# Expert 0's first tile built from one-hot products and an early gather, and routing groups of 4 and 2 tiles, in an attention, mixture-of-experts and feed-forward chain

## The chip, the cores and the metric

The kernel runs on one core of one Trainium2 chip. The metric is the device time of one execution in microseconds (us), the median of several runs; less is better. Times inside the kernel come from one profiled execution and count from its first instruction.

## The reference

```python
attn = softmax(q @ k.T / 8 where 0 <= i - j < 64) @ v      # 4 x 8 x 576 x 64
x = attn as rows                                             # 2304 x 512
compute = x @ w_skip > 0                                     # the other rows stay as they are
e = argmax(x @ w_gate); gate = softmax(x @ w_gate)[e]        # 8 experts
x = x + gate * (relu(x @ w1[e]) @ w2[e])                     # 512 -> 1024 -> 512
h = x @ w_in                                                 # 512 -> 2048
g = h if h >= 1, 0 if h <= -1, else (h + 1) ** 2 / 4
out = g @ w_out                                              # 2048 -> 512
```

All arrays are fp32. With the inputs of the test the experts get 63, 85, 141, 113, 265, 116, 58 and 62 rows.

## The kernel before

The work has three stages, one behind the other, and the program text is the order on every engine.

**Attention and routing (0 to about 110 us).** The 2304 rows are 18 tiles of 128 tokens. Each tile t goes through the score products (`stage_s`, L338, softmax on VectorE and ScalarE), the transposes of the weights (`stage_t`, L363, copied to pts by ScalarE and VectorE, L367 and L369), the value products (`stage_v`, L388, which read v from the four buffers vt and end in x, scaled by VectorE at L394 to L396), a store of x to DRAM (x1), the transposes of x (`stage_x`, L409), and the gate products (`stage_l` L430, `stage_l2` L449). The loop runs them as a pipeline, several tiles at a time; the last tiles are written out by hand behind it (L642 to L696). Tiles are routed in six groups of three (`ROUTES`). `route_a` (L457 to L470, six VectorE operations) chooses each token's expert as a one-hot row oh; `route_b` (L484 to L519) ranks tokens within the expert by products of triangular and ones matrices, on top of the counts so far (run); `route_h` (L547, L549) makes from a rank two one-hot matrices (to, at), `route_c` (L564) multiplies them and adds up (acc, in the end idx at L571), the list of row numbers by expert and slot; `route_g` (L530 to L533) makes the gate and stores it beside x in x1, from ScalarE's queue. 120 spare products of ones (`keep_warm`, L444) stand among the last groups' steps, in batches of 6, 14, 20 and 80; 69 (L586) stand at the start of the program.

**Experts (116.5 to 271 us).** `fetch` gathers 128 rows of x1 with their gates by an indirect DMA of POOL (L715; an expert's tile t with column e·18+t of idx), `prep` transposes them (L733) and splits them into a high and a low half (L131 ScalarE, L132 VectorE), `ffn` does the two products (L759 ha and hb, L798 y) in three passes of high and low halves, `store_x` writes the rows back by an indirect DMA of POOL (L724), with small memsets (tick) that keep scatters and gathers apart. Every expert has a first tile; the second and the third run inside `tc.If` on the counts, which each engine reads into registers (L833, cnt_i). `fetch(e, 2)` stands at the start of the second tile. Expert e's hooks, called within `ffn`, prepare the next expert and split weights.

**Weights.** They come as raw tiles (L115 wu, L118 wd), at most `most` at a time, from SP's or ScalarE's queue, and ScalarE (L136) and POOL or VectorE (L137) split each into a pair in a ring of 14. Before, `most` is 2 in the loop and 6 from t = 14 on, so that raw loads go out while attention still loads vt from SP's queue (L305).

**Dense stage (271 to 701 us).** Six blocks of 384 rows, products L922 and L950 one behind the other.

## Time and profile before

| | |
|---|---|
| runs of the kernel | 708.78, 703.59, 702.24 us; median 703.59 |
| the profiled execution | 703.17 us, of which 701.5 are the span from the first to the last instruction |
| TensorE busy | 674.2 us of the span, 96% |
| VectorE, ScalarE, POOL busy | 425.6, 385.9, 90.7 us |
| mean granted TensorE clock | 0.992 |
| first product of expert 0 (ha) | 116.53 us |
| start of the dense stage | 271.35 us |

In rows of the timeline the first number is the start and the second the length in us; then engine, line, operation, the tiles written and read, the number of instructions, and in brackets the idle time of the engine before it and what ended it. PE is TensorE, PEld its weight loads, DVE VectorE, ACT ScalarE; an engine's name with a q is its sequencer, which issues DMAs. [...]

### The profile page before, as it was taken

The numbers are of one execution on the slowest core, as the hardware profiler recorded it, in microseconds if no ns is written. First come the engines' busy times: TensorE is split into PE (matmuls) and PEld (weight loads), VectorE is DVE, ScalarE is ACT, GpSimd is POOL, SyncE is SP. The second block draws the span as 40 slices with busy tenths as digits, with TensorE's granted clock in tenths as the row PEclk, the third lists the DMA queues.
The fourth block names the chain that finished last, engine by engine and source line by source line (L and its number), as shares of the span: only waits on it lengthen the run. The fifth ranks groups of instructions, "written<-read, shape, count | busy, mean of one in ns | idle before, by whom it ended". The sixth has DMA issues, their size and how long they took to land.

```text
span 701.5 us, 12250 instructions
## 1 busy us (share of the span) xinstructions
PE 674.2 (96%) x4630; PEld 575.6 (82%) x4630; DVE 425.6 (61%) x808; ACT 385.9 (55%) x768; POOL 90.7 (13%) x137
## 2 busy tenths in 40 slices
PE   7999989999998998999999999999999999999997
PEld 6777778776776765987989999999999999999995
DVE  4888864897781799787888854444433433433332
ACT  5887742583751764566766655454444454445443
POOL 3255545222210221000000000000000000000000
PEclk9999998999999999999999999999999999999999
DMA  8999953897891693442333202121300030001001
GB/s 259 288 272 290 307 133 115 289 329 275 267 357 31 205 332 95 172 127 84 121 92 96 69 0 61 31 60 31 91 1 0 1 91 0 1 1 45 1 1 45
DMA packets 34504, 88.83 MB, mean 127 GB/s; under 512 B 6958, under 2 KB 8110, under 8 KB 34420
## 3 DMA queue, kind: packets, MB, share of 16 engines
q1 hardware_dynamic: 26208, 73.82, 34.3%
q10 hardware_dynamic: 5892, 7.35, 3.1%
q0 software_dynamic: 2320, 6.58, 2.8%
q8 instruction: 48, 0.79, 0.5%
q14 instruction: 36, 0.29, 0.1%
HBM read 75.65 MB, written 13.12 MB: 127 GB/s over the span
## 4 chain that ended last, share of the span: by engine, by line
PE 55%; DVE 3%; ACT 1%; issue 1%; ACTq 0%; DVEq 0%
PE h L922 27%; PE po L950 26%; PE spare L1038 1%; PE p2x L912 1%; DVE c L943 1%; DVE c L940 1%; ACT q L933 1%; DVE w L137 1%; DVE gs L941 0%; DVE q L932 0%; DVE x2T L132 0%; ACT q L929 0%; DVE q L936 0%; ACT part L959 0%; ACT w L136 0%
## 5 line engine op out<-in xcount | busy, mean ns | idle before, releaser
L922 PE MATMUL h<-x2T,w 128*128 128x384 f32 x1152 | 218.0, 337 | 1.1 <-DVE x2T L132 0.9
L950 PE MATMUL po<-w,gs 128*128 128x512 f32 x864 | 217.3, 395 | 1.7 <-ACT w L136 0.9
L922 PEld LDWEIGHTS h<-x2T,w 128*128 128x128 f32 x1152 | 204.6, 188 | 10.0 <-DVE x2T L132 1.7
L950 PEld LDWEIGHTS po<-w,gs 128*128 128x128 f32 x864 | 159.5, 188 | 32.3 <-ACT w L136 1.2
L929 ACT ACTIVATE q<-h 128x384 f32<-128x384 f32 x96 | 47.0, 489 | 108.1 <-PE h L922 104.2
L932 DVE TENSOR_SCALAR q<-q 128x384 f32<-128x384 f32 x96 | 34.4, 358 | 98.2 <-ACT q L929 98.0
L936 DVE TENSOR_TENSOR q<-hs,q 128x384 f32<-128x384 f32 x96 | 53.7, 559 | 49.8 <-ACT q L933 49.8
L938 ACT ACTIVATE gs<-q 128x384 fp32r<-128x384 f32 x96 | 50.4, 525 | 60.0 <-DVE q L936 60.0
L941 DVE TENSOR_TENSOR gs<-q,gs 128x384 fp32r<-128x384 f32 x96 | 53.6, 559 | 44.4 <-ACT gs L938 44.4
L136 ACT ACTIVATE w<-raw 128x1024 fp32r<-128x1024 f32 x64 | 65.3, 1056 | 18.7 <-PEq L869 4.7
L798 PE MATMUL y<-w,hT 128*128 128x512 f32 x264 | 70.2, 403 | 4.1 <-DVE hT L132 2.8
L137 DVE TENSOR_TENSOR w<-raw,w 128x1024 fp32r<-128x1024 f32 x55 | 64.8, 1219 | 3.8 <-ACT w L136 1.9
L933 ACT ACTIVATE q<-q 128x384 f32<-128x384 f32 x96 | 50.5, 526 | 22.2 <-DVE q L932 18.6
L798 PEld LDWEIGHTS y<-w,hT 128*128 128x128 f32 x264 | 47.3, 188 | 17.3 <-DVE hT L132 4.5
L349 ACT ACTIVATE pr<-s,nb 128x128 f32<-128x128 f32 x144 | 39.2, 384 | 16.5 <-DVE nb L345 16.5
L931 ACT ACTIVATE hs<-h 128x384 f32<-128x384 f32 x96 | 46.7, 487 | 0.0
L759 PE MATMUL ha<-w,mxT 128*128 128x512 f32 x132 | 35.3, 416 | 3.7 <-ACT mxT L131 1.5
L759 PEld LDWEIGHTS ha<-w,mxT 128*128 128x128 f32 x132 | 25.1, 197 | 13.2 <-issue 4.5
L759 PE MATMUL hb<-w,mxT 128*128 128x512 f32 x132 | 35.2, 402 | 0.0
L345 DVE TENSOR_REDUCE nb<-s 128x4 f32<-128x512 f32 x36 | 23.2, 686 | 16.0 <-PE s L338 14.5
L724 POOL DMA_INDIRECT x<-mx,idx x11 | 16.5, 1501 | 115.6 <-POOLq L865 60.4
L131 ACT ACTIVATE hT<-hTp 128x512 fp32r<-128x512 f32 x22 | 13.2, 599 | 27.1 <-PE hTp L772 13.0
(170 smaller groups left out, 702.1 us busy)
## 6 DMA issues: line engine op xcount, KB each, us to landing
raw<-in_wu SPq DMA_DIRECT2D x61, 512.0 KB, 6.0
raw<-in_wd SPq DMA_DIRECT2D x31, 512.0 KB, 4.0
x<-x SPq DMA_DIRECT2D x22, 256.0 KB, 3.2
vt<-in_vs SPq DMA_DIRECT2D x36, 130.0 KB, 6.2
out<-out SPq DMA_DIRECT2D x36, 128.0 KB, 2.4
x<-x ACTq DMA_DIRECT2D x17, 256.0 KB, 6.6
q<-in_qs SPq DMA_DIRECT2D x8, 512.0 KB, 5.0
kt<-in_ks SPq DMA_DIRECT2D x8, 512.0 KB, 6.2
```

Of the source, the lines that this page charges most:

```text
L136: nc.scalar.activation(t[:, 0], src, AF.Copy)
L137: eng.tensor_tensor(t[:, 1], src, t[:, 0].bitcast(F32), ALU.subtract)
L759: nc.tensor.matmul(ph, lhsT=xT[:, a, c, :], rhs=halves[4 * e + j, c][:, b, :], start=(n == 0), stop=(n == len(seq) - 1),)
L798: nc.tensor.matmul(py, lhsT=hT[j][:, a, c, :], rhs=halves[4 * e + 2 + j, c][:, b, :], start=(j == 0 and n == 0), stop=(j == 1 and n == len ...
L922: nc.tensor.matmul(ph, lhsT=halves[U_IN + m // 4, c][:, b, (m % 4) * P : (m % 4 + 1) * P], rhs=xT[:, a, c, :], start=(n == 0), stop=(n == ...
L929: nc.scalar.activation(q, ph, AF.Relu, bias=0.5, scale=0.5)
L931: nc.scalar.activation(h, ph, AF.Copy)
L933: nc.scalar.activation(q, q, AF.Square)
L936: nc.vector.tensor_tensor(q, h, q, ALU.max)
L938: nc.scalar.activation(gs[:, 0], q, AF.Copy)
L941: dve.tensor_tensor(gs[:, 1], q, gs[:, 0].bitcast(F32), ALU.subtract)
L950: nc.tensor.matmul(po[i], lhsT=gs[:, a, i * P : (i + 1) * P], rhs=w[:, b, :], start=(m == m0 and (a, b) == PASSES[0]), stop=(m == m1 - 1 a ...
```

## The change

Expert 0's first tile no longer waits for idx and a gather. Its transposed rows are summed in one PSUM bank (mpx_0, tag s0) from fp32 products. For tiles 13 to 17 x is still in SBUF (13 and 14 in a part of kt that is free by then): `add_rows` multiplies it with a selector, the one-hot matrix of "this token has rank j in expert 0" (`choose`). For the first 13 tiles the rows come by an indirect gather of POOL that is issued as soon as the first four groups' list stands (`gather_ahead`), into a buffer set to zero before, and are added by a product with the identity.

For this the groups are 3, 3, 3, 4, 2 and 3 tiles (`ROUTES`), and the fourth group, tiles 9 to 12, is routed between the value products of tile 15 and the transposes of tile 16. All spare products of the routing's end go. The 69 warm products of ones, bf16, 108 columns, become 11 of the identity, fp32, 192 columns. `most` is 2 until t = 14, then 3, and 6 only behind the last gates, where the loads go out from ScalarE's queue. The counts are read on each engine ahead of the split of expert 0's tile; expert 1's gather goes out before expert 0's (which still brings its rows for the sum at its end), and VectorE's next weight splits stand behind both. `fetch(e, 2)` moves from the start of the second tile into the first tile's hook, right behind the second tile's transposes.

```diff
-ROUTES = (3, 3, 3, 3, 3, 3)
-WARM = 69
-WARM_COLUMNS = 108
+ROUTES = (3, 3, 3, 4, 2, 3)
+WARM = 11
+WARM_COLUMNS = 96
-KEEP = (14, 20, 80, 6, 36)
+KEEP = 36
+KEPT_AT = {13: (2, 0), 14: (2, 512)}
+ROWS_AT = (0, 0)
+SEL_AT = ((1, 0), (1, 128), (1, 256), (1, 384), (1, 512))
...
+        def choose(t, i):
+
+            sel = kept(*SEL_AT[t + i - t0], P)
+            nc.vector.tensor_scalar(
+                sel, slot_r[:, 0], st["ps", t][:, i : i + 1], 0.0, op0=ALU.add, op1=ALU.is_equal
+            )
+            return sel
+
+        def gather_ahead():
+
+            at = sm.tile([P, 1], I32, tag="ahead", name="ahead", bufs=1)
+            nc.vector.tensor_copy(at, acc[:, 0:1])
+            nc.gpsimd.indirect_dma_start(
+                out=rows, out_offset=None, in_=x1[0 : t0 * P], in_offset=bass.IndirectOffsetOnAxis(ap=at, axis=0),
+                bounds_check=t0 * P - 1, oob_is_err=False,
+            )
+
+        def add_rows(px, x, sel, first=False, last=False):
+            for c in range(KD):
+                nc.tensor.matmul(
+                    px[:, c, :], lhsT=x[:, c * P : (c + 1) * P], rhs=sel,
+                    start=(first and c == 0), stop=(last and c == KD - 1),
+                )
...
-        warm = psp.tile([P, P], F32, tag="o", name="warm")
+        warm = psp.tile([P, H, P], F32, tag="o", name="warm")[:, 0:2, 0:WARM_COLUMNS]
         for _ in range(WARM):
-            nc.tensor.matmul(warm[:, 0:WARM_COLUMNS], lhsT=ones, rhs=ones[:, 0:WARM_COLUMNS], start=True, stop=True)
+            nc.tensor.matmul(
+                warm, lhsT=ident, rhs=ident[:, 0:WARM_COLUMNS].rearrange("p (o k) -> p o k", o=1).to_broadcast([P, 2, WARM_COLUMNS]),
+                start=True, stop=True,
+            )
...
-            most[0] = 1 if t < 3 else 2 if t + 4 < NT else RAWS[0] + RAWS[1]
+            most[0] = 1 if t < 3 else 2 if t + 3 < NT else 3
...
         stage_x(NT - 4)
+        tp, (ip, m, side) = of[NT - 6][0], of[NT - 6][1:]
+        assert ip == m - 1 and not due and not gates
+        route_a(tp, m)
         stage_v(NT - 3)
         store_t(NT - 3, nc.sync)
+        route_b(tp, m, side)
+        route_g(tp, m)
+        route_h(tp, m, range(1, m))
+        route_h(tp, m, [0], dve)
         stage_t(NT - 2)
         stage_t(NT - 1)
-        ranks[0]()
         stage_v(NT - 2)
...
         stage_x(NT - 3)
-        stage_l(NT - 4)
+        stage_l2(NT - 4, *of[NT - 4][1:])
+        n0, n = ROUTES[-2:]
+        route_a(t0, n0)
         stage_x(NT - 2)
+        route_c(tp, m)
+        gather_ahead()
         stage_x(NT - 1)
...
+        route_b(t0, *of[t0][2:])
+        sels = [choose(t0, i) for i in range(n0)]
         stage_l(NT - 3)
...
-        keep_warm(KEEP[3])
         stage_l2(NT - 1, *of[NT - 1][1:])
-        route_g(t0, of[t0][2])
-        for f in later:
-            f()
+        route_p(t0, n0)
+        route_h(t0, n0)
         route_a(t1, n)
-        route_h(t0, of[t0][2], [n - 1])
+        x0 = bank("s0", "mpx0_0")
+        for i in range(n0):
+            add_rows(x0, xs_late[t0 + i], sels[i], first=(i == 0))
+        route_g(t0, n0)
         route_g(t1, n)
-        keep_warm(KEEP[0])
+        most[0] = RAWS[0] + RAWS[1]
+        load_raws(nc.scalar)
         route_b(t1, *of[t1][2:])
-        route_h(t1, n)
-        route_c(t0, of[t0][2])
+        add_rows(x0, rows, ident)
+        sels += [choose(t1, i) for i in range(n)]
+        nc.vector.tensor_tensor(cnt_i, st.pop("cn"), base[:, 0], ALU.subtract)
+        for i in range(n):
+            add_rows(x0, xs_late[t1 + i], sels[n0 + i], last=(i == n - 1))
+        route_p(t1, n)
+        route_h(t1, n, [0])
+        route_h(t1, n, range(1, n), dve)
+        route_c(t0, n0)
         route_c(t1, n)
...
+        _, counts = nc.values_load_multi_w_load_instructions(cnt_i[0:1, 0:NE], min_val=0, max_val=N)
+        xeT[0, 0] = prep(None, "0_0", px=x0)
+        fetch(1, 0)
         fetch(0, 0)
 
         nc.gpsimd.memset(tock, 0.0)
         nc.vector.tensor_copy(tick_seen, tock)
         work(splits, [dve] * 2)
-        pre(0, 0)
...
-        _, counts = nc.values_load_multi_w_load_instructions(cnt_i[0:1, 0:NE], min_val=0, max_val=N)
...
                     prep(xe[e, 1], f"{e}_1", "mxTl", xeT[e, 1])
+                    fetch(e, 2)
...
             with tc.If(counts[e] > P):
-                fetch(e, 2)
                 tile_of(e, 1)
```


Three places show what that does to the order. TensorE at the end of the routing, before: rk_end are the rank products of the last group, misc the list, spare the products of ones, mpx_0 the transposes of expert 0's gathered rows, ha its first product.

```order
L509 MATMUL rk_end<-run,ones 128x9
L444 MATMUL spare<-ones 128x128
...
L564 MATMUL misc<-at_2181,to_2179 128x144
...
L564 MATMUL misc<-at_2247,to_2245 128x144
L444 MATMUL spare<-ones 128x128
...
L733 MATMUL mpx_0_2373<-ident,mx_0_2362 128x128 x4
L833 TENSOR_LOAD cnt_i
L759 MATMUL ha_0_2475<-w_0_472,mxT_0_2378 128x512 x4
```

After, lg_end are the last logits; in mpx_0's rows the operands are selectors in kt and x of tiles 13 and 14 (in kt) or 15 to 17 (x_…), and with ident the gathered rows:

```order
L459 MATMUL lg_end<-quarters,ls_2089 128x9
L561 MATMUL mpx_0_2119<-kt 128x128 x8
L495 LDWEIGHTS stri
...
L520 MATMUL rk_end<-run,ones 128x9
L561 MATMUL mpx_0_2119<-ident,kt 128x128 x4
L561 MATMUL mpx_0_2119<-kt,x_1871 128x128 x4
L561 MATMUL mpx_0_2119<-kt,x_1961 128x128 x4
L561 MATMUL mpx_0_2119<-kt,x_1993 128x128 x4
L599 MATMUL misc<-at_2101,to_2099 128x144
...
L599 MATMUL misc<-at_2193,to_2191 128x144
L873 TENSOR_LOAD cnt_i
L811 MATMUL ha_0_2325<-w_0_417,mxT_0_2294 128x512 x4
```

The 24 products of L561 stand in the place of the spare products and of the four transposes, eight of them ahead of the rank products; the register load now stands right ahead of ha.

VectorE between the value products of tiles 15 and 16, before: den, rec and x are tile 15's scaling, pts the copy of tile 16's transposed weights, r, ps and rc the ranks of tiles 9 to 11.

```order
L394 TENSOR_SCALAR den_1931<-o_1930 128x8
L395 RECIPROCAL rec_1932<-den_1931 128x8
L396 TENSOR_TENSOR x_1933<-o_1930,rec_1932 128x512
L369 COPY pts_1968<-pt_1963 128x512
L512 TENSOR_TENSOR r_9_1990<-misc,oh_1834 128x27
L514 TENSOR_REDUCE ps_1992<-r_9_1990 128x3
L516 SCALAR_TENSOR_TENSOR rc_1994<-ps_1992,far 128x3
L519 SCALAR_TENSOR_TENSOR rc_1994<-rc_1994,ps_1992 128x3
L394 TENSOR_SCALAR den_1998<-o_1997 128x8
```

After, with the gate (sx, gate) and one pair of one-hot matrices (to, at) of tiles 9 to 12:

```order
L407 TENSOR_SCALAR den_1869<-o_1868 128x8
L408 RECIPROCAL rec_1870<-den_1869 128x8
L409 TENSOR_TENSOR x_1871<-o_1868,rec_1870 128x512
L522 TENSOR_TENSOR r_9_1903<-misc,oh_1862 128x36
L524 TENSOR_REDUCE ps_1905<-r_9_1903 128x4
L534 SCALAR_TENSOR_TENSOR rc_1907<-ps_1905,far 128x4
L537 SCALAR_TENSOR_TENSOR rc_1907<-rc_1907,ps_1905 128x4
L570 TENSOR_REDUCE sx_1910<-ex_136 128x4
L572 RECIPROCAL gate_1912<-sx_1910 128x4
L583 TENSOR_SCALAR to_1927<-slot_r,rc_1907 128x128
L585 TENSOR_SCALAR at_1929<-slot_c,rc_1907,val 128x144
L379 COPY pts_1943<-pt_1938 128x512
```

Ranks, gate and list of the fourth group have moved ahead of the copy of pts; six operations of its choice stand right ahead of these rows.

SP's queue at tiles 14 to 16, before: raw are weights, vt the values of attention.

```order
L115 DMA raw_0_1510<-in_wu 128x1024
L305 DMA vt_160<-in_vs 64x520
L305 DMA vt_161<-in_vs 64x520
L115 DMA raw_2_1631<-in_wu 128x1024
L115 DMA raw_0_1633<-in_wu 128x1024
L115 DMA raw_2_1635<-in_wu 128x1024
L115 DMA raw_0_1637<-in_wu 128x1024
L305 DMA vt_158<-in_vs 64x520
L305 DMA vt_159<-in_vs 64x520
```

After:

```order
L119 DMA raw_0_1455<-in_wu 128x1024
L313 DMA vt_163<-in_vs 64x520
L313 DMA vt_164<-in_vs 64x520
L313 DMA vt_161<-in_vs 64x520
L313 DMA vt_162<-in_vs 64x520
L119 DMA raw_2_1668<-in_wu 128x1024
L119 DMA raw_0_1670<-in_wu 128x1024
L313 DMA vt_163<-in_vs 64x520
L313 DMA vt_164<-in_vs 64x520
```

The four raw loads ahead of vt_158 and vt_159 are gone, and two stand behind the pair that answers to it.

## Rows read from the trace of the kernel before

**Rows 1.** The page's chain that ended last, by line

```profile
PE h L922 27%; PE po L950 26%; PE spare L1038 1%; PE p2x L912 1%; DVE c L943 1%; DVE c L940 1%; ACT q L933 1%; DVE w L137 1%; DVE gs L941 0%; DVE q L932 0%; DVE x2T L132 0%; ACT q L929 0%; DVE q L936 0%; ACT part L959 0%; ACT w L136 0%
```

**Rows 2.** Windows: stretch and length (us), busy us (instructions) by engine, PEclk, DMA share, GB/s

```profile
102.05:108.80 6.75, 6.39 (x63) 6.39 (x64) 4.23 (x23) 2.72 (x6) 3.66 (x6) 0.54 0.10 3
117.00:210.00 93.00, 88.58 (x415) 69.04 (x414) 74.53 (x93) 53.80 (x70) 23.67 (x38) 1.00 0.88 303
210.00:220.00 10.00, 7.56 (x28) 5.66 (x27) 1.44 (x2) 1.20 (x2) 1.08 (x2) 0.83 0.24 60
```

**Rows 3.** Line 586: ns min/median/max, first and last start; then the timeline's first score product

```profile
L586 PE MATMUL warm<-ones x69: 211/296/296, 1.1 to 7.1; 128*128 128x108 bf16 x69
...
7.69 0.99 PE L338 MATMUL s<-kt,q 64*64 64x128 f32 x28
```

**Rows 4.** Timeline 71 to 88 us (start, length, instruction, idle before): SP's loads, value products

```profile
71.84 5.65 SPq L115 DMA_DIRECT2D raw<-in_wu  x4
...
85.95 0.30 PE L388 MATMUL o<-vt,pts 128*64 128x65 f32 x2 [1.26 <-DMA vt<-in_vs]
...
86.54 1.15 PE L388 MATMUL o<-vt,pts 128*64 128x65 f32 x30 [0.28 <-DMA vt<-in_vs]
```

**Rows 5.** Timeline 90 to 99 us: tile 16's last copy; value products of tiles 16 and 17

```profile
93.64 0.69 DVE L369 COPY pts<-pt 128x512 f32<-128x512 f32 x1
...
94.43 1.15 PE L388 MATMUL o<-vt,pts 128*64 128x65 f32 x32
...
96.53 1.12 PE L388 MATMUL o<-vt,pts_last 128*64 128x65 f32 x30 [0.26 <-DMA vt<-in_vs]
```

**Rows 6.** Timeline 104 to 117 us: from the last choice to expert 0's first products

```profile
103.77 0.54 PE L449 MATMUL lg_end<-quarters,ls 128*128 128x9 f32 x2
...
105.63 0.19 DVE L470 TENSOR_TENSOR oh<-desc,pick 128x27 bf16<-128x27 f32 x1
...
110.01 0.31 DVE L571 TENSOR_TENSOR idx<-misc,acc 128x144 int32<-128x144 f32 x1 [1.10 <-PE misc L564]
...
111.22 1.23 POOL L715 DMA_INDIRECT mx<-x,idx  x1 [1.88 <-DVE cnt_i L573]
...
112.65 2.34 DVE L137 TENSOR_TENSOR w<-raw,w 128x1024 fp32r<-128x1024 f32 x2
112.75 3.06 POOL L715 DMA_INDIRECT mx<-x,idx  x1 [0.18 <-issue]
...
115.09 0.63 PE L733 MATMUL mpx<-ident,mx 128*128 128x128 f32 x4 [0.64 <-DVE w L137]
...
116.53 0.73 PE L759 MATMUL ha<-w,mxT 128*128 128x512 f32 x2 [0.81 <-ACT mxT L131]
```

**Rows 7.** Lines 444, 833 (ns min/median/max); landing of the DMAs of 715, then 533

```profile
L444 PE MATMUL spare<-ones x120: 219/219/330, 103.2 to 114.2; 128*128 128x128 bf16 x120
...
L833 PEldq TENSOR_LOAD <-cnt_i x1: 780/780/780, 115.1 to 115.1; - x1
...
DMA to landing us min/median/max: 3.7/7.2/9.1
...
DMA to landing us min/median/max: 2.0/4.4/9.8
```

**Rows 8.** Timeline 73 to 77 us: transposes, 128 columns each

```profile
74.06 0.66 PE L409 MATMUL px<-ident,x 128*128 128x128 f32 x4
...
75.73 1.09 PE L363 MATMUL pt<-ident,pr 128*128 128x128 f32 x8
```

**Rows 9.** Timeline 170 to 175 us, another tile, and 207 to 219 us, expert 4's third

```profile
171.55 3.06 PE L759 MATMUL ha<-w,mxT 128*128 128x512 f32 x12 [0.43 <-PEq L869]
...
208.43 0.98 POOL L715 DMA_INDIRECT mx<-x,idx  x1 [0.24 <-issue]
...
213.19 0.63 PE L733 MATMUL mpx<-ident,mx 128*128 128x128 f32 x4 [1.75 <-DMA mx<-x,idx]
214.50 4.60 PE L759 MATMUL ha<-w,mxT 128*128 128x512 f32 x12 [0.69 <-ACT mxT L131]
```

More of the change, by code (lines that the diff above doesn't have):

```diff
@@ L264, in moe_chain @@
     nc.gpsimd.memset(far, FAR)
-    exs = [const.tile([P, n, NE + 1], F32, name=f"ex{i}") for i, n in enumerate(ROUTES[:3])]
+    exs = [const.tile([P, max(ROUTES), NE + 1], F32, name=f"ex{i}") for i in range(3)]
     for ex in exs:
@@ L326, in stage_s @@
             e, o = place[e % 4], place[o % 4]
-            s = [psp.tile([P, 4, P], F32, tag=f"s{(2 * t + k) % 3}", name=f"s{2 * t + k}") for k in range(2)]
+            s = [bank(f"s{(2 * t + k) % 3}", f"s{2 * t + k}") for k in range(2)]
             for k in range(2):
@@ L360, in stage_t @@
                 pr = st.pop(("p", g))
-                pt = psp.tile([P, 4, P], F32, tag=f"s{k}" if last else f"pt{k}", name=f"pt{g}")
+                pt = bank(f"s{k}" if last else f"pt{k}", f"pt{g}")
                 for p in range(4):
@@ L439, in stage_l @@
             st["ls", t] = ls
-        def keep_warm(n):
-            spare = psp.tile([P, P], F32, tag="o", name="spare")
-            for _ in range(n):
-                nc.tensor.matmul(spare, lhsT=ones, rhs=ones, start=True, stop=True)
         def stage_l2(t, i, n, side):
@@ L728, in store_x, with prep @@
             apart(dma, "scatters", ("scatters", "gathers"))
-        def prep(x, name, tag="mxT", into=None):
-            px = bank(3 if tag == "mxT" else 7, [P, KD, P], f"mpx{name}")
-            for c in range(KD):
-                nc.tensor.transpose(px[:, c, :], x[:, c * P : (c + 1) * P], ident)
+        def prep(x, name, tag="mxT", into=None, px=None):
+            if px is None:
+                px = bank(3 if tag == "mxT" else 7, [P, KD, P], f"mpx{name}")
+                for c in range(KD):
+                    nc.tensor.transpose(px[:, c, :], x[:, c * P : (c + 1) * P], ident)
             if into:
```

116 lines of the change are left out of this document (59 added, 57 removed).

## Prediction

> **What bounds the kernel now.** I read the stretches first, then the chain that ended last, then the time order around each place that the diff touches. The chain [rows 1] consists of TensorE lines of the last stage (L922, L950) and of little else, and TensorE works without a gap of note from 271.35 us, where that chain begins, to the end. So that stage keeps its length, and a change in front of it moves the end one for one as far as it moves the last expert's last product. In front of it three stretches count: the attention (TensorE full), the end of the routing from 98 to 116.5 us, and the experts, 11 tiles of 128 rows one behind the other. For each edit the question is therefore by how much it moves the first expert's first product (ha, L759, at 116.53 us, the last row of [rows 6]) and whether an expert tile gets shorter.
>
> The reader is to see three things. The attention loses 1.54 us near its end to a transfer: the value products of one tile wait 1.26 and 0.28 us for vt [rows 4], because SP was held for 5.65 us by four raw loads that stand ahead of vt in its queue. The routing's end [rows 6] is a chain of small steps, not of work: the choice oh is done at 105.82, the list idx at 110.32, the gather is issued at 111.22, its rows are transposed at 115.09, and ha starts at 116.53. [...] One expert tile is longer than the others too: the third tile of expert 4 waits 1.75 us for a gather that POOL issued behind the store of the first tile, and runs its first product group at less than the full clock [rows 2, 9].
>
> **The change part by part**
>
> Start. The warm products wait for ident (POOL, done at about 1.37 us) where they waited for ones: they start at 1.40 in place of 1.12. One has 192 columns in fp32, and the trace of before has none. Transposes give a price: eight of 128 columns take 1.09 us, four 0.66 [rows 8], so 0.107 for one more; an fp32 product is shown as two records (L449 has 30 for 15 tiles) where a transpose is one, so 128 columns cost about 0.215 us at the high clock and 0.43 at the low one, 192 columns 0.32 and 0.64. Before, the clock rose at about 6.9 us (a warm product takes 296 ns until then, 211 after [rows 3]). If it does so again, 8.6 of the 11 are done by then and 2.4 follow in 0.8: the mask product starts at 7.7 in place of 7.16 and the first score product 0.59 later, at 8.3, where it stood at 7.69 behind the scaled q [rows 3]. Cost +0.5 us; bounds 0 (q is late anyway) and +1.3 (no rise: 7.0 us of warm products).
>
> Raw loads. With `most` at 2 and 3 the four loads ahead of vt are gone from SP; two come a tile later. The wait of 1.54 us goes [rows 4]: −1.5; bounds −1.5 and 0 (another transfer is late in its place). Both terms together: attention 1.0 us earlier.
>
> Fifth and sixth group, up to the last choice. Now VectorE is what is late. Ahead of the pts copy of tile 16 it has the old x of tile 15 and in addition the six operations of the choice (about 0.2 us each, 1.3), four of the rank (0.9), two of the gate (0.4) and one pair for the list (0.63). The oh of [rows 6] took 0.19, which with the gap to the next makes the 0.2. The copy, which ended at 94.33 before [rows 5], ends at about 96.4 even with 1.0 gained, so the value products of tile 16 start at 96.5 where they started at 94.43 [rows 5]. From the end of tile 17's value products to the last logit it took 6.66 us before, 97.65 to 104.31 [rows 5, 6], with a group's choice and ranks, ten operations of about 0.21 from start to start, on VectorE in between; ScalarE's copies of the last logits stood behind these. Without them I count 4.6. Tile 17's value products follow those of tile 16 and end at 100.0, so the last logit stands at 104.6. The last choice is then done at 106.2.
>
> Expert 0's first tile. Removed from the path: the rest of the list, its issue, its landing and its transposes, from 105.82 to 115.72. Added: 24 fp32 products into one bank. Eight (tiles 13 and 14) stand before the rank products, four (the gathered rows) and twelve (tiles 15 to 17) behind. At the high clock: eight by 106.4, rank products by 107.1, ranks 107.6, three selectors (0.28 each) by 108.5, the four rows products meanwhile, twelve in 2.6 by 110.7, the hi copy (0.6) by 111.5. The five list products that stand in TensorE's row behind them end at about the same time, then comes the counts' register load, which before was hidden while TensorE waited for the gather and now is on the path with 0.78 us [rows 7]: ha at 112.3. If the clock is low from 104.6 on, the eight take 3.4, the four 1.7, the twelve 5.2, and the list and its load stand behind: ha at 117.8. Before, the clock fell at about 102 and came back at about 108.8, 6.8 us later [rows 2], on about the same activity; here it would come back near 111, and ha falls to about 114.9. I take 113.8, between the high case and this one: −2.7 against 116.53. Bounds −4.2 and +1.3.
>
> The gather ahead needs the stored x of the first 13 tiles and the gates of tiles 9 to 12, and VectorE's list; it is issued at about 103.2. Before, the first one took 3.9 us from issue to the transposes that used it [rows 6], and a landing took 3.7 to 9.1 us [rows 7]; so 107.1, as the rank products end. That hides it, by little: a landing of 7.2 us, the median, makes ha 2 to 3 us later. The gate's own store took 2.0 to 9.8 us to land [rows 7] and starts near 95.5, so at its longest it ends at 105.3.
>
> Beside this stands a row on POOL: the second gather took 3.06 us, while VectorE subtracted raw weights for 2.34 from 112.65, where the first took 1.23 [rows 6] and one among the experts 0.98 [rows 9]. [...] The change also moves VectorE's two subtractions behind both first gathers, which takes that 3.06 away; nothing on TensorE waits for it.
>
> Expert 4's third tile. Its gather is now issued in the first tile's run, some 13 us before. What is left is the branch, 0.43 us as at another branch [rows 9], in place of 1.75: −1.3. The clock then need not fall: its first twelve products took 4.60 us where they take 3.06 behind that other branch [rows 9]; −1.54. Together −2.9; bounds −1.3 and −2.9. The other experts have no third tile.
>
> The raw loads that leave the attention (pairs 12 and 13 and one of wd, 128 x 1024 x 4 B each, 1.57 MB) now go out near 107, in a stretch in which the queues moved 3 GB/s [rows 2]. That idle stretch hides them; if it didn't, they cost 5.2 us at the 303 GB/s of the experts' stretch [rows 2].
>
> **Sum.** Start and vt are inside ha's time. −2.7 −2.9 = −5.6 against the profiled execution's 703.17, which gives 697.6. The median of the runs is 703.59, 0.42 above it: **698.0 us**, −0.8%.
>
> **Rivals**
>
> Everything at the high clock, and the gather early: ha at 112.3, −4.2 −2.9 = −7.1, so 696.5; if the warm products cost nothing either, 696.0. For it: 8 products that keep TensorE busy where it waited before. Against it: the clock fell at 102 with TensorE busy for nine tenths of the time that followed [rows 2], and the spare products that stood against that are all gone.
>
> The clock stays low to the experts, or the gather lands late: ha at 116 to 117.8, only the third tile is gained: 703.59 −0.5 −2.9 = 700.2 to 703.59 +1.3 −2.9 = 702.0. For it: the clock of the routing's end [rows 2] and the 120 spare products that go. [...] Against it: the fp32 products fill that time themselves.
>
> Slower: the raw stream becomes the bound of the first expert. The loads held back (`most` 3) are needed by pairs 12 to 15, the experts' stretch has a DMA share of 0.88 [rows 2], so what is lost is not made up until about 210 us, and the 5.2 us come on TensorE as waits before y of expert 0 or ha of expert 1. ha's gain then is eaten (−2.7 +5.2), the third tile starts later by as much and gains only the 1.3 of the wait: 703.59 +1.2 = 704.8. It decides if the loads issued near 107 land after about 118. Against it: an idle stretch of 5 us and more.
>
> That the change doesn't do what it says: expert 0's tile is read in two ways, the rows products wait for the gather; if that is at 111 the whole is the second rival.
>
> **How the numbers follow.** Forecast 45%, high clock 30%, low clock or late gather 18%, slower 7%. A measurement of this kernel can tell about 1% from no change, so faster means below 696.55. The first rival and a part of the forecast's spread lie there: 0.33; above 710.6 lies next to nothing but mishaps of the raw stream that go beyond its 5.2: 0.04; the rest, 0.63, within 1%. The range holds from 2 us below the best case, for the terms priced from neighbours, to the low clock's end: 693.9 to 702.4.
>
> **What would show it right or wrong.** Right: vt waits at line 388 gone; ha at 113 to 114.5; a register load of 0.7 to 0.8 us right before it on TensorE; the third tile's transposes behind a wait of 0.4 to 0.5, its twelve products in about 3.06; the last stage as long as before. Wrong: the rows products waiting for the gather ahead, waits of y or ha for raw loads in expert 0 and 1, a granted clock near 0.5 from 104 us to the experts, or a score product at line 338 that starts later than 8.5.

## The result, and the profile after

The changed kernel took 694.77 us (median of four runs, 693.14 to 695.51), the kernel before 703.68 on the same chip (four runs): ratio 0.9858 [0.9814, 0.9902], 8.9 us less. A second comparison later gave 696.48 against 702.91, 0.9897 [0.9861, 0.9933]. The forecast was 698.0, no change that a measurement can tell: it is faster, by 1.4% and by 1.0% in the two comparisons. The profiled execution took 693.14 us, the lowest of the changed kernel's ten runs (their median is 695.4), against 703.17; its dense stage starts (with its first spare products) at 261.51 where it started at 271.35, so 9.84 of the 10.03 us arise ahead of that stage.

The page's chain that ended last still consists of the dense stage's two product lines, 25% and 25% (L975 and L1003 are L922 and L950 of [rows 1]):

```profile
PE po L1003 25%; PE h L975 25%; DVE c L996 2%; PE spare L1091 1%; ACT q L986 1%; DVE gs L994 1%; PE p2x L965 1%; DVE c L993 1%; DVE w L141 1%; DVE q L985 1%; DVE q L989 1%; DVE x2T L136 0%; ACT q L982 0%; ACT gs L991 0%; DVE c_first L996 0%
```

Windows of the kernel after (stretch and length, busy us and instructions of PE, PEld, DVE, ACT and POOL, the granted clock, DMA share, GB/s), to set beside [rows 2]:

```profile
98.00:102.00 4.00, 3.10 (x47) 2.59 (x41) 2.95 (x15) 1.79 (x4) 0.14 (x1) 1.00 0.36 135
102.00:106.00 4.00, 4.00 (x55) 3.62 (x48) 2.74 (x17) 1.06 (x5) 3.95 (x5) 1.00 0.10 25
106.00:110.00 4.00, 3.88 (x35) 3.72 (x33) 2.17 (x12) 0.47 (x1) 1.77 (x4) 1.00 0.67 73
...
117.00:210.00 93.00, 87.73 (x410) 68.11 (x410) 74.96 (x93) 52.59 (x69) 24.94 (x38) 1.00 0.85 298
210.00:220.00 10.00, 9.51 (x46) 7.49 (x45) 2.46 (x4) 3.22 (x5) 0.48 (x1) 1.00 0.01 2
```

TensorE is busy for all of 102 to 106 and 3.88 of the 4 us behind it, at the full clock; before, 102.05 to 108.8 ran at 0.54. The stretch 210 to 220 is at 1.00 in place of 0.83. The granted clock is a share of TensorE's full speed. Before, it was 0.50 from 102.57 to 109.39, where spare products of 128 columns started 107 ns apart, and 1.00 behind that, where they started 56 ns apart.

The warm products (ns min, median, max), with the first score product of the timeline, as [rows 3]:

```profile
L616 PE MATMUL warm<-ident x22: 326/326/688, 1.4 to 6.4; 128*128 128x192 f32 x22
...
7.08 1.10 PE L348 MATMUL s<-kt,q 64*64 64x128 f32 x32
```

Value products of tiles 14 to 17 and VectorE's copy of pts for tile 16, timeline (start, length), as [rows 4, 5]:

```profile
84.41 1.15 PE L401 MATMUL o<-vt,pts 128*64 128x65 f32 x32
...
89.25 1.15 PE L401 MATMUL o<-vt,pts 128*64 128x65 f32 x32
...
94.06 0.68 DVE L379 COPY pts<-pt 128x512 f32<-128x512 f32 x1
...
94.80 1.22 PE L401 MATMUL o<-vt,pts 128*64 128x65 f32 x32 [1.17 <-ACT pts L377]
...
97.10 1.15 PE L401 MATMUL o<-vt,pts_last 128*64 128x65 f32 x32
```

No bracket names vt any more: that wait is gone. Two others stand in its place, both from the routing of tiles 9 to 12: TensorE waits 1.16 us for their choice oh ahead of tile 16's transposes, and tile 16's products wait 1.17 us for pts. VectorE's half of pts ends at 94.74 and ScalarE's, which the label names, at 94.75: the issue of the gate's store stands ahead of it in ScalarE's row and waits for VectorE's gate.

```profile
91.56 0.18 PE L495 MATMUL misc<-oh,stri 128*128 128x36 bf16 x1 [1.16 <-DVE oh L480]
...
93.67 0.38 ACTq L573 DMA_DIRECT2D x<-gate  x1
...
94.15 0.60 ACT L377 ACTIVATE pts<-pt 128x512 f32<-128x512 f32 x1 [2.98 <-DVE at L585]
```

The end of the routing, timeline, as [rows 6]:

```profile
101.86 1.29 POOL L554 DMA_INDIRECT kt<-x,ahead  x1 [4.14 <-DVE r L522]
...
104.54 0.24 DVE L480 TENSOR_TENSOR oh<-desc,pick 128x27 bf16<-128x27 f32 x1
...
105.46 1.14 PE L561 MATMUL mpx<-ident,kt 128*128 128x128 f32 x8
...
106.44 2.93 PE L561 MATMUL mpx<-kt,x 128*128 128x128 f32 x24
...
109.12 0.76 PE L599 MATMUL misc<-at,to 128*128 128x144 f32 x5
...
109.53 0.60 ACT L135 ACTIVATE mxT<-mpx 128x512 fp32r<-128x512 f32 x1 [5.40 <-PE misc L599]
...
109.92 0.31 DVE L603 TENSOR_TENSOR idx<-misc,acc 128x144 int32<-128x144 f32 x1 [1.65 <-PE misc L599]
...
110.33 2.99 PE L811 MATMUL ha<-w,mxT 128*128 128x512 f32 x12 [0.45 <-DVE idx L603]
...
113.50 2.34 DVE L141 TENSOR_TENSOR w<-raw,w 128x1024 fp32r<-128x1024 f32 x2
113.62 3.05 POOL L766 DMA_INDIRECT mx<-x,idx  x1 [0.19 <-issue]
```

The last choice is done at 104.78 (105.82 before). The four products of the gathered rows start at 105.46, the twelve of tiles 15 to 17 at 106.44, the hi half is copied by 110.13, the list idx is done at 110.23, and ha starts at 110.33 where it started at 116.53. TensorE's register load and the landing of the gather ahead, to set beside [rows 7]:

```profile
L873 PEldq TENSOR_LOAD <-cnt_i x1: 776/776/776, 109.0 to 109.0; - x1
...
DMA to landing us min/median/max: 3.5/3.5/3.5
```

The load starts at 109.0 and ends at 109.78, while the five list products run (109.12 to 109.88): it holds up nothing. Expert 4's third tile, as [rows 9]:

```profile
204.91 0.60 PE L785 MATMUL mpx<-ident,mx 128*128 128x128 f32 x4
206.20 3.07 PE L811 MATMUL ha<-w,mxT 128*128 128x512 f32 x12 [0.69 <-ACT mxT L135]
```

The transposes wait for nothing, and the twelve products take 3.07 us where they took 4.60.

### The profile page after: what moved, and what is told of

The parts are those of the page before. It is cut to its first block, busy times and chain, and to the rows that moved or that the text cites. A ratio compares the mean times of both kernels' runs of the same rounds, so it can differ in the third digit from the quotient of the medians.

```text
span 691.4 us, 12027 instructions
## 1 busy us (share of the span) xinstructions
PE 665.6 (96%) x4505; PEld 567.9 (82%) x4505; DVE 427.3 (62%) x814; ACT 386.0 (56%) x769; POOL 93.4 (14%) x140
## 4 chain that ended last, share of the span: by engine, by line
PE 52%; DVE 6%; ACT 2%; issue 1%; ACTq 0%; DVEq 0%
PE po L1003 25%; PE h L975 25%; DVE c L996 2%; PE spare L1091 1%; ACT q L986 1%; DVE gs L994 1%; PE p2x L965 1%; DVE c L993 1%; DVE w L141 1%; DVE q L985 1%; DVE q L989 1%; DVE x2T L136 0%; ACT q L982 0%; ACT gs L991 0%; DVE c_first L996 0%
## 5 line engine op out<-in xcount | busy, mean ns | idle before, releaser
L975 PE MATMUL h<-x2T,w 128*128 128x384 f32 x1152 | 218.0, 337 | 1.1 <-DVE x2T L136 1.1
L1003 PE MATMUL po<-w,gs 128*128 128x512 f32 x864 | 217.0, 395 | 1.6 <-ACT w L140 0.9
L975 PEld LDWEIGHTS h<-x2T,w 128*128 128x128 f32 x1152 | 204.5, 188 | 10.0 <-DVE x2T L136 1.7
L1003 PEld LDWEIGHTS po<-w,gs 128*128 128x128 f32 x864 | 159.5, 188 | 32.1 <-ACT w L140 1.2
L811 PE MATMUL ha<-w,mxT 128*128 128x512 f32 x132 | 33.4, 399 | 3.6 <-DVE mxT L136 0.7
L811 PEld LDWEIGHTS ha<-w,mxT 128*128 128x128 f32 x132 | 23.8, 188 | 12.3 <-issue 4.7
L811 PEld LDWEIGHTS hb<-w,mxT 128*128 128x128 f32 x132 | 24.0, 188 | 4.7
```

The source lines that it names most:

```text
L811: nc.tensor.matmul(ph, lhsT=xT[:, a, c, :], rhs=halves[4 * e + j, c][:, b, :], start=(n == 0), stop=(n == len(seq) - 1),)
L975: nc.tensor.matmul(ph, lhsT=halves[U_IN + m // 4, c][:, b, (m % 4) * P : (m % 4 + 1) * P], rhs=xT[:, a, c, :], start=(n == 0), stop=(n == ...
L1003: nc.tensor.matmul(po[i], lhsT=gs[:, a, i * P : (i + 1) * P], rhs=w[:, b, :], start=(m == m0 and (a, b) == PASSES[0]), stop=(m == m1 - 1 a ...
```

## The experiments

Runs of one job share the runs of the kernel before; "ratio" is to these, with its 95% interval. "Before + ..." and "after + ..." name the kernel that was edited. Where runs of two jobs are compared, the kernel before had medians of 702.18 to 703.83 in them.

**e1_third: the third tile's gather alone (before + one edit).**

```diff
                     prep(xe[e, 1], f"{e}_1", "mxTl", xeT[e, 1])
+                    fetch(e, 2)
...
-                fetch(e, 2)
                 tile_of(e, 1)
```

> The kernel before with one edit: the gather of an expert's third tile is issued in the hook of the first tile. If the wait and the clock behind it make up the term (my theory), the third tile's transposes start 0.4 to 0.5 us behind y, its twelve first products take about 3.06 in place of 4.60, and the median falls by 2.9 to 3.4 us, to about 700.5. Rival: the gather is only issued earlier and the store it now stands ahead of, or the branch, takes the time back; then the median moves by less than 1 us.

701.71 us (10 runs) against 703.83, ratio 0.9955 [0.9921, 0.9989]. Third tile, timeline:

```profile
213.99 0.60 PE L733 MATMUL mpx<-ident,mx 128*128 128x128 f32 x4
215.28 3.06 PE L759 MATMUL ha<-w,mxT 128*128 128x512 f32 x12 [0.69 <-ACT mxT L131]
```

The wait of 1.75 is gone and the products take 3.06: 3.3 us in its profile, 2.1 in the medians. The counter-proof is **e15_third_old** (after, this edit undone):

> The changed kernel with the third tile's gather at the start of the second tile again. If the term is as large as in the kernel before, the transposes wait 1.7 to 1.8 us for the gather, the twelve products behind take about 4.6 us, and the median is 3.0 to 3.5 us above the changed kernel's of this job, at 697.5 to 698.5. Rival: with the raw loads further behind in the new kernel the gather comes at another time and the wait is below 1 us; then less than 1.5 us.

698.91 (12 runs) beside 696.48 (6) for the changed kernel in the same job, **e14_after**, 2.4 us:

> The changed kernel once more, for a second profile and more times. If its order keeps the clock up, the granted clock is 1.00 from 91 to 117 us again and ha stands 12.0 to 12.3 us behind the end of tile 17's value products (12.08 in its first profile); if that was chance, the clock is below 0.8 in some stretch and ha is 2 to 4 us later. Median 694 to 696.

```profile
208.57 0.63 PE L785 MATMUL mpx<-ident,mx 128*128 128x128 f32 x4 [1.85 <-DMA mx<-x,idx]
209.89 3.07 PE L811 MATMUL ha<-w,mxT 128*128 128x512 f32 x12 [0.69 <-ACT mxT L135]
```

The wait is back, with 1.85 us, but the products behind it kept the full clock. So the wait is the part of this term that both profiles have, and the 1.5 of the clock comes only where the clock falls in that wait (0.83 from 210 to 220 before, 1.00 in e15).

**e2_warm, e6_warm34, e9_oldwarm: the warm products.** e2_warm is before with 11 fp32 products of 192 columns in place of the 69; e9_oldwarm is after with the old 69; e6_warm34 is e2 with 34 products of 62 columns. e2's edit:

```diff
-WARM = 69
-WARM_COLUMNS = 108
+WARM = 11
+WARM_COLUMNS = 96
...
-            nc.tensor.matmul(warm[:, 0:WARM_COLUMNS], lhsT=ones, rhs=ones[:, 0:WARM_COLUMNS], start=True, stop=True)
+            nc.tensor.matmul(warm, lhsT=ident, rhs=..., start=True, stop=True)
```

> The kernel before with one edit: 11 fp32 products of the identity in place of 69 bf16 products of ones at the start. The changed kernel's trace has the first score product at 7.08 us where it was 7.69. Theory A (fp32 products of the identity raise the clock earlier): first score product again at about 7.1, median lower by about 0.6 us. Rival B (the number of products alone, the loads of q came earlier by chance): the first score product stays at 7.6 to 7.7 and the median does not move.

719.58 (4 runs) against 703.83, ratio 1.0241 [1.0191, 1.0292]: nothing like it was expected. The first score product came early enough, at 7.24. The time went in TensorE's sequencer, at the branches between the experts (line 868: ns min, median, max of eight branches), and then as idle time ahead of an expert's ha:

```profile
L868 PEldq COMPARE_BRANCH  x8: 73/4218/5335, 128.0 to 283.2; - x8
...
132.84 3.03 PE L762 MATMUL ha<-w,mxT 128*128 128x512 f32 x12 [2.56 <-PEq L868]
```

In the kernel before the same branch (line 865) has a median of 368 ns, in the one after 325 (line 919):

```profile
L865 PEldq COMPARE_BRANCH  x8: 73/368/451, 127.9 to 268.1; - x8
```

```profile
L919 PEldq COMPARE_BRANCH  x8: 73/325/436, 121.6 to 258.1; - x8
```

Nothing at the branches was edited; 58 products fewer stand at the start of the program. e9_oldwarm does the reverse, more products ahead of the branches of the changed kernel:

> The changed kernel with the 69 bf16 warm products of ones again: 94 TensorE instructions more ahead of the experts. Theory (the price of an expert branch hangs on where the code lies, and the change's own count keeps it where it was): branches at 3 to 5 us on TensorE for six experts, median 706 to 713. Rival (the slow branches belong to the kernel before or to the gather): branches below 0.5 us, median 694 to 696.

713.06 (4 runs), ratio 1.0136 [1.0083, 1.0190], again with slow branches; expert 1's ha waits 4.53 us for one.

```profile
L916 PEldq COMPARE_BRANCH  x8: 73/4295/6633, 123.7 to 278.2; - x8
```

e6_warm34 has about the work of e2 at the start, in about as many instructions of TensorE as the kernel before:

```diff
-WARM = 69
-WARM_COLUMNS = 108
+WARM = 34
+WARM_COLUMNS = 31
```

> The kernel before with 34 fp32 products of the identity of 62 columns at the start: the same columns as the 11 of the change, but as many instructions (136 for 138) as the 69 bf16 products had. Theory (only the number of instructions made the run with 11 slow): branches at 0.07 to 0.45 us, median 703 to 704.5. Rival (the warm products of the identity or their kind make it slow): median 715 to 720.

714.07 (4 runs), ratio 1.0121 [1.0060, 1.0182]. The branches were fast, as expected, and the time was not, for another cause:

```profile
L868 PEldq COMPARE_BRANCH  x8: 73/408/451, 138.3 to 278.5; - x8
...
L586 PE MATMUL warm<-ident x68: 421/421/474, 1.4 to 15.8; 128*128 128x62 f32 x68
```

All 68 records of its warm products take 421 to 474 ns, from 1.42 to 16 us; the first score product came at 16.97 where it came at 7.69, and expert 0's ha at 126.95 where it came at 116.53. That is nearly all of the 10.7 us.

So the price of a branch depends on what stands ahead of it in the program. Counted by the records of weight loads and products ahead of expert 0's ha, the median is 0.33 to 0.41 us at 3658 (before), 3656 (e6), 3408 (after) and 3416 (e5 below), and 3.6 to 4.3 us at 3564 (e2), 3320 (e4 below) and 3502 (e9). What goes on during a slow branch is in the traces too. The queue that the profile calls instruction (q8) moves pieces of 16 KiB. In e2, e4 and e9 such a piece starts to move inside 20 of TensorE's 21 branches that are longer than 1 us, and the branch ends 1.1 to 1.5 us after the piece has landed; in the other fourteen profiles none starts inside any branch of TensorE. e2's first slow branch runs from 128.00 to 132.66; the piece moves from 129.9 to 131.2.

That such a branch waits for the piece is read from these times; no run shows it by itself. What sets a slow count apart from a fast one is not shown by seven of them; that the price hangs on how many products stand ahead and not on what they compute is, by e2 and e6 (medians of 4.22 and 0.41 us), and by e4 and e5 below (3.58 and 0.33).

**e3_loads: the raw loads held back alone (before + one edit).**

```diff
-            most[0] = ... 2 if t + 4 < NT else RAWS[0] + RAWS[1]
+            most[0] = ... 2 if t + 3 < NT else 3
...
         route_g(t1, n)
+        most[0] = RAWS[0] + RAWS[1]
+        load_raws(nc.scalar)
```

> The kernel before with one edit: at most 2 and then 3 raw tiles until the last gates, and the held back loads from ScalarE's queue behind them. Theory: the waits of 1.26 and 0.28 us for vt go, the value products of tile 16 start 1.5 us earlier, and so does the last choice; but the first expert still waits for its gather, so ha moves by about 1.5 and the median by -1.5. Rival: the late loads collide with the gather or make the experts wait: median between 0 and +5 us.

703.96 (10 runs) against 703.83, ratio 0.9998 [0.9962, 1.0033]. The wait of tile 14 for vt is gone and the last value products end at 95.09 (97.65 before), but ha starts only 2 us earlier than before and its first eight records alone take 3.69 us:

```profile
113.19 0.63 PE L735 MATMUL mpx<-ident,mx 128*128 128x128 f32 x4 [2.45 <-issue]
...
114.56 3.69 PE L761 MATMUL ha<-w,mxT 128*128 128x512 f32 x8 [0.74 <-ACT mxT L131]
...
110.00:117.00 7.00, 3.82 (x24) 2.96 (x22) 2.28 (x3) 0.60 (x1) 4.47 (x8) 0.83 0.76 225
```

With the old gather behind it, the end of the attention gives its gain back. The loads that were held back go out from 103.81 on, ahead of the gather, which now takes 5.39 us from its issue to the transposes where it took 3.87 (111.22 to 115.09); TensorE stands still until 113.19, and the granted clock is 0.83 from 110 to 117.

```profile
107.80 1.23 POOL L717 DMA_INDIRECT mx<-x,idx  x1 [2.00 <-ACT w L136]
```

So this is the rival of the expectation, a collision with the gather, as far as one profile shows. Undone in the changed kernel (**e10_oldloads**) the same edit shows:

> The changed kernel with the raw loads as before: up to six raw tiles from tile 14 on, none held back. Theory: tile 14's value products wait for vt again (1 to 2 us), everything behind that is as much later, and the gather and its products are not touched: ha 1 to 2 us later, median 696 to 697. Rival: the early loads give back at the experts what they cost in the attention: median 694 to 695.

697.83 (10 runs) against 702.18, ratio 0.9931 [0.9902, 0.9960], 2.4 us more than the changed kernel's 695.4 (by the ratios to each job's kernel before, 2.4 to 5.1), and the wait is back:

```profile
90.52 1.54 PE L401 MATMUL o<-vt,pts 128*64 128x65 f32 x32 [1.01 <-DMA vt<-in_vs]
```

**e4_gather, e5_gather_fill, e11_fill_oldloads: expert 0's tile by list and gather again.** e4 is after without selectors, sums, gather ahead, and with the old gather of expert 0; e5 is e4 + 24 products of the identity where the sums stood; e11 is e5 with the old loads.

```diff
-        gather_ahead()
-        add_rows(x0, rows, ident)
-            add_rows(x0, xs_late[t1 + i], sels[n0 + i], last=(i == n - 1))
-        xeT[0, 0] = prep(None, "0_0", px=x0)
-        fetch(1, 0)
         fetch(0, 0)
+        fetch(1, 0)
...
+        pre(0, 0)
```

e5 adds 8 of these products behind the choice of the last group and 16 behind the counts (x0 is read by nothing):

```diff
+                nc.tensor.matmul(x0[:, i % 4, :], lhsT=ident, rhs=ident, start=True, stop=True)
```

> The changed kernel with expert 0's first tile made from the list and its gather again, without one-hot products and gather ahead, and without any spare product. Theory A (the 24 fp32 products keep the clock up): the granted clock falls below 0.7 between 102 and 112 us, ha starts at 116 to 118 and the median is 700.5 to 702. Theory B (the clock stays up because the waits ahead of 102 us are shorter): the clock stays at 0.9 or more, idx stands at about 109, ha starts at 114.5 to 115.5 and the median is 699 to 700.

721.39 (4 runs), ratio 1.0255 [1.0188, 1.0322]. Two prices are in it: slow branches, and a clock of 0.50 from 106 us on, where TensorE is busy for 1.53 of 4 us and then not at all until the gather lands:

```profile
L908 PEldq COMPARE_BRANCH  x8: 73/3581/5655, 132.5 to 282.5; - x8
...
106.00:110.00 4.00, 1.53 (x5) 1.00 (x4) 2.07 (x10) 1.07 (x2) 1.70 (x4) 0.50 0.57 42
...
117.94 1.09 PE L774 MATMUL mpx<-ident,mx 128*128 128x128 f32 x4 [8.44 <-DMA mx<-x,idx]
```

> The changed kernel with expert 0's first tile made from the list and its gather again, and 24 fp32 products of the identity with itself in the places where the one-hot products stood, so that TensorE's instructions up to the experts are as many as in the changed kernel, to within eight. Theory (the 2 to 5 us that TensorE spent at expert branches in the run without the products come from where the instructions lie): branches back at 0.07 to 0.45 us, the experts as in the changed kernel, ha at 117 to 119.5 because the gather lands late beside the raw loads, median 702 to 704. Rival (the branches wait for something that the gather's order sets): they still take 3 to 5 us and the median is 718 or more.

707.81 (10 runs) against 703.33, ratio 1.0063 [1.0032, 1.0094]. With 24 products that compute nothing new, 13.6 us of e4's time are gone:

```profile
L914 PEldq COMPARE_BRANCH  x8: 73/331/412, 133.9 to 270.6; - x8
...
106.00:110.00 4.00, 4.00 (x43) 4.00 (x39) 1.85 (x9) 1.16 (x2) 1.61 (x4) 1.00 0.57 45
...
111.60 1.23 POOL L761 DMA_INDIRECT mx<-x,idx  x1 [2.75 <-ACT w L140]
...
118.10 1.09 PE L780 MATMUL mpx<-ident,mx 128*128 128x128 f32 x4 [7.75 <-issue]
```

The branches are fast again, and the clock holds to 110: in this order products in that place keep it, whether they compute the tile or not (e12 below shows that they do not in every order). The list's gather is then on the path with 6.5 us (111.60 to 118.10), and the clock falls in that wait (0.89 from 110 to 117). Beside it the sums as such are worth 707.81 − 695.4 = 12.4 us. A part of the 6.5 was the loads held back, which now go out ahead of the gather:

> Both undone: expert 0's first tile from the list and its gather, 24 products of the identity in the place of the one-hot products, raw loads as before. In the run with the held back loads the gather took about 6.5 us from issue to transposes and the first twelve products of expert 0 ran below the full clock. Theory (the loads that go out at 107 share the DMA queues with that gather): 3.7 to 4 us from issue to transposes again, ha at 115 to 117, median 701.5 to 704. Rival (the gather is late for another reason): 6 us and more, median 706 to 708.

```profile
116.32 1.24 POOL L759 DMA_INDIRECT mx<-x,idx  x1 [2.75 <-DVE idx L603]
...
120.23 1.08 PE L778 MATMUL mpx<-ident,mx 128*128 128x128 f32 x4 [5.14 <-issue]
```

With these loads back in the attention the gather takes 3.9 us. The median is 705.94 (10 runs), ratio 1.0052 [1.0015, 1.0089]; against e10_oldloads, which differs by the sums, 8.1 us more. It is also 3.8 us more than the kernel before (702.18), although its third tile's gather goes out early, which alone gave 2.1. So the regrouping, the loss of the spare products and the new warm products cost some 6 us by themselves (an estimate, 3.8 and 2.1), and the sums have to earn that first: 3.8 up, 8.1 down by the sums and 2.4 down by the loads make the 6.8 between 702.18 and 695.4.

**e7_later, e8_later_rows, e12_v3: what is the new wait for pts worth?** e7 is after with the fourth group's choice and ranks behind the transposes of tile 16; e8 is e7 with the gathered rows' products last; e12 moves the ranks behind tile 16's value products, rows last too.

```diff
-        route_a(tp, m)
         stage_v(NT - 3)
...
-        route_b(tp, m, side)
...
         stage_t(NT - 2)
+        route_a(tp, m)
         stage_t(NT - 1)
+        route_b(tp, m, side)
```

> The changed kernel with the fourth group's choice, ranks, gate and list behind the transposes of tile 16 instead of ahead. VectorE then copies pts before it routes: the value products of tile 16 start at 92.5 to 93 us where they start at 94.80 in the changed kernel, and the gather ahead, which is issued behind tile 16's x, stays at about 102 or comes 1 us earlier. Theory: ha 1 to 2 us earlier, median 693 to 694. Rival: POOL's pairs of the fourth group end later and hold its list, the gather ahead and the rows products, and the time is given back: median 694.5 to 696.

695.65 (4 runs), ratio 0.9862 [0.9806, 0.9918]: no difference that four runs can tell. In its profile one wait of 1.24 us for the choice oh takes the place of the two of 1.16 and 1.17, and from tile 15's value products to the end of tile 17's it takes 8.05 us in place of 9.00; counted from the first score product, ha comes 102.82 us later, in the changed kernel 103.25. So the gain is there with up to 1 us, and the medians do not resolve it.

> As the run before, and the products of the gathered rows behind those of tiles 15 to 17 instead of ahead, so that a late gather is hidden by 12 more products. If the gather ahead is what is late in the run before, ha is 0.5 to 2 us earlier than there; if not, the same within 0.2 us, and the median 693 to 694.

695.97 (4 runs), ratio 0.9876 [0.9820, 0.9931]: the rows products were not waited for in e7 either, so nothing could be gained there. In this profile the clock fell ahead of the sums (0.76 from 98 to 102).

> The changed kernel with the fourth group's choice behind the transposes of tile 16, its ranks, gate and list behind the value products of tile 16, and the gathered rows' products last. In the run with the ranks ahead of those value products TensorE waited 1.24 us there for VectorE. Theory: this wait goes, tile 17's values end 1.5 to 2.5 us earlier than in the changed kernel counted from the first score product, ha 1 to 1.5 us earlier, median 693 to 694. Rival: POOL's pairs end later and the list holds ha: median 694.5 to 696.

697.85 (12 runs) against 702.18, ratio 0.9932 [0.9904, 0.9960], some 2 us slower than the changed kernel. Its profile, the slowest of the twelve runs (703.33), shows TensorE waiting more from 98 to 102 (busy 2.02 of 4 us) and then half the clock:

```profile
98.00:102.00 4.00, 2.02 (x30) 1.72 (x32) 1.91 (x9) 0.28 (x1) 3.28 (x8) 0.77 0.37 117
102.00:106.00 4.00, 3.79 (x31) 3.27 (x28) 2.56 (x12) 1.41 (x3) 1.68 (x3) 0.50 0.17 66
```

The sums' first 16 records start at 110.09, still at half the clock (0.52 from 110 to 114), and take 3.76 us where they take 2.03 in the changed kernel. So the sums held a clock that was up (1.00 from 102 to 110 in the changed kernel); they did not keep one from falling ahead of them. Whether the median's 2 us have this cause is not shown.

**e13_before and e14_after: how often does the clock fall?**

> The kernel before once more, for a second profile of its own routing end. If the clock that fell at 102 us in the first profile belongs to this order of work, it is below 0.7 from 102 to 108 again; if it falls in some executions only, as two runs of this order with another edit suggest (1.00 there), it can stay at 1.00, and expert 0's first product then stands about 17.3 us behind the end of tile 17's value products where it stood 18.9 behind it.

One more profile of the kernel before took 706.40 us:

```profile
106.00:110.00 4.00, 4.00 (x43) 4.00 (x43) 2.08 (x11) 0.50 (x2) 2.72 (x4) 0.50 0.06 0
...
106.00:110.00 4.00, 4.00 (x46) 3.98 (x45) 3.36 (x19) 0.00 (x0) 2.15 (x4) 1.00 0.41 13
```

The clock is low again in the kernel before (first row; ha at 119.61) and full in the changed one (second row; ha at 112.08). e6 (0.63 from 112 to 116 there, 0.52 from 116 to 120) lost it too; e1 and e2, with the same order here, kept it (1.00 from 91 to 117 in e1; six spare products took 0.49 us from 104.61 on in e2, 0.80 from 103.17 on in the kernel before). So the order of before lost it in three of five profiles (and in e3, with other loads, in part: 0.71 from 102 to 106), and why in these and not in the others stays open; the changed kernel's order kept it from 91 to 117 us in all five profiles that have it, its own and those of e9, e10, e14 and e15.

## Why the prediction was wrong, and where it was right

The parts came as described, and one step between them did not: the clock. ha moved by −6.20 us where −2.7 were forecast, and the third tile by −3.49 where −2.9 were (from the start of the y in front of it to its hb: 207.48 to 218.94 before, 201.13 to 209.10 after).

**The step that failed** is "I take 113.8, between the high case and this one". The forecast let the clock fall near 104.6 and come back near 111. It never fell: the sums lie where TensorE waited, and e4 and e5 show that in this order products in their place hold it (0.50 without them and 1.00 with them from 106 to 110). That a product takes twice as long at the low clock was an estimate: spare products show 1.9 (107 and 56 ns apart), and the sums' first 16 records 1.85 (3.76 us in e12, 2.03 in the changed kernel). From the end of tile 17's value products to ha the prediction's two values were 13.8 and, at the high clock, 12.3; 12.08 were measured, and 12.74 to 12.80 in e9, e10, e14 and e15. ha came 3.47 us ahead of the 113.8 forecast: 1.72 of them lie in this stretch, 1.11 at the start and 0.64 in VectorE's row, both below. This is the first rival, "Everything at the high clock", with its 696.5; it had 30%. What spoke against it there, that the clock fell at 102 "with TensorE busy for nine tenths", does not carry over from one order to another, and not even from one run of the same order to the next. Of the 6.8 us that this stretch got shorter (18.88 to 12.08), the clock is some 1.5: in e1 and e2, with the old path at the full clock, it took 17.40 and 17.29.

**Its parts.** The last logit stood 5.19 us behind tile 17's value products where 4.6 were counted. The twelve products took 2.93 and not 2.6, a price that was too low by an eighth. The register load, put "on the path with 0.78 us", costs nothing: the sequencer runs it, from 109.0 to 109.78, beside the list products of 109.12 to 109.88. The gather ahead was issued at 101.86 (103.2 forecast), landed 3.5 us later, at about 105.4, and was hidden by little, as forecast: its products start at 105.46. In e9, e10, e14 and e15 the margin is 0.8 to 1.0.

**VectorE's row.** Value products of tile 15 to the end of those of tile 17: 9.64 forecast, 9.00 measured, 6.29 before. The row takes less than counted: the choice, priced at 1.3, puts the scaling of tile 15 back by 0.94 (den starts 2.17 us behind the start of tile 15's value products in place of 1.23), and ranks, gate and pair take 1.60 in place of 1.93. What the row does to TensorE are the two waits of 1.16 and 1.17.

**Start.** +0.5 forecast, −0.61 in this pair (7.69 to 7.08); by luck. The five profiles with the old warm products show the first score product at 6.59 to 7.69 (mean 7.30), the eleven with the 11 fp32 products at 7.05 to 8.61 (mean 7.71). On average +0.4, about as priced. What varies is how soon the records of the warm products get shorter: the eleven products take 5.3 to 6.8 us together, and the first score product stands 0.4 behind their end each time.

**Raw loads.** −1.5 forecast and −1.50 measured (tile 15's value products came 83.67 us behind the first score product, now 82.17). That agreement to the hundredth is luck, since the profiles show 83.67 to 87.90 with the old loads and 81.60 to 86.01 with the new ones, much of it from the first 50 us. Nearer to the term is the time from tile 13's value products to tile 15's: 9.98 us in all ten profiles with the new loads, 11.37 to 14.39 in the seven with the old ones (11.88 before). So the term is there in every profile, with 1.4 us at least and 1.90 in this pair. The cover held: no ha or y waits for a raw load. That rival, 704.8, did not come; e5 and e11 show where it could have: a gather behind these loads takes 2.6 us longer.

**Third tile.** The wait of 1.75 and the clock's 1.5 went as forecast. Not even the 0.43 of the branch is left: it takes 0.07 us at 201.74, beside the products of y (201.13 to 205.07). In e15 the wait is 1.85 and the clock stays, and the medians differ by 2.4.

**Sum.** −6.20 and −3.49 are 9.69 of the 9.84 us at the start of the dense stage. The profiled execution was the changed kernel's fastest, with the start's luck in it; the median of its ten runs, 695.4, is 2.6 us below the forecast. One rival was missing altogether: that the number of instructions removed changes what every later branch costs. e2, e4 and e9 show that it decides over 10 us and more; the changed kernel happens to stand at a count where the branches stay fast.

## What to carry to other kernels

A step that waits for a list, its transfer and its transposes can be replaced by products that build the same rows from what is on the chip, and it can pay twice, where TensorE then keeps its clock (1.00 from 102 to 110 here, 0.54 from 102.05 to 108.8 before); price such a stretch at both clocks and look for what fills its gaps rather than at when the clock fell before. After an edit that adds or removes instructions ahead of branches, read the branch rows of the sequencer before anything else: their price can outweigh the edit (e2: 15.8 us more, where 0.6 less was expected). Single profiles of one kernel differ by over a microsecond at the start, by over three in the attention (tile 15's value products at 83.67 and 87.09 behind the first score product, in the two of the kernel before) and by the clock of a whole stretch, so take a term from two of them, and between two marks close to it.

## What the runs showed of the hardware

- A branch on TensorE's sequencer cost 0.32 to 0.41 us (median of eight) in some kernels and 3.6 to 4.3 us, up to 6.6, in others, with the same branches and the same code behind them (e2 against e6, e4 against e5). 20 of the 21 branches longer than 1 us have a 16 KiB piece on the instruction queue starting inside them; no branch of a kernel with fast branches has one.
- 68 records of fp32 products of 62 columns (e6) ran for 14.8 us at 421 to 474 ns each without getting faster, and the 32 score products behind them took 1.98 us where they take 1.10 in the kernel before; 22 records of 192 columns (after) went from 688 to 326 ns within 5 us. The granted clock reads 1.00 in both stretches, so at the start the level has to be read from durations.
- An indirect gather took 6.5 us from issue to its transposes behind five raw weight loads that were issued in the 5 us ahead of it (e5), 5.4 behind three (e3), and 3.9 behind two (e11) and behind none (before).
- VectorE's two subtractions again stand beside one slow gather: 3.05 us for the issue at 113.62, where the two ahead of it took 1.06 and 0.95, while VectorE ran 2.34 from 113.50. The prediction expected this price to go; it moved to a later gather, for which nothing waits. The same pair stands in e1, e9, e13 and e14 (3.05 or 3.06 us each); in e3 and e5 the issue beside the two subtractions (2.36 us) took 1.95 and 1.93. Why it takes longer there is not shown.
